# Three pairs of token tiles formed by seven block products each, with attention packed into the tiles ahead of them

## The chip, the cores and the metric

The kernel runs on one core of a Trainium2 chip. The metric is the device time of one execution in microseconds (us). Before the change the median of three runs is 853.47 us (853.21 to 854.79). About 0.2% (1.7 us) is what a measurement of this kernel can tell from no change.

## The reference

A linear attention over 8 batches, 8 heads, 576 positions and 64 features per head is followed by a two-layer network with a squared ReLU:

```python
q_s = exp(q - max(q, -1));  q_s /= sum(q_s, -1) + 1e-9      # over the 64 features
k_s = exp(k - max(k, 2));   k_s /= sum(k_s, 2) + 1e-9       # over the 576 positions
kv  = einsum('bhsd,bhse->bhde', k_s, v)
x   = einsum('bhsd,bhde->bhse', q_s, kv)   # as 4608 tokens x 512
h   = maximum(x @ w_in, 0)                 # 512 -> 2048
out = (h * h) @ w_out                      # 2048 -> 512
```

## The kernel before

Tokens are taken in nine tiles of 512. Tiles 0 to 7 hold the first 512 positions of batches 0 to 7, tile 8 gathers the last 64 positions of every batch. Every float32 operand of the network is held as a rounded high part and a rest, and each product of 128x128 by 128x512 is three matmuls (high by high, high by rest, rest by high). The weights arrive as 64-bit words and are turned into such parts during tile 0 (`scale_words`, `join_words`, `split_words`).

An ordinary tile (the loop `for t in range(WT)`, L1590, with WT = 7, so tiles 0 to 6) runs 16 columns f. `first` (L1049) forms one 128x512 piece of h from four 128-row pieces of x: 12 matmuls. ScalarE takes the ReLU (`r`), VectorE the product of h and r, ScalarE the square as the high part (`gh`), VectorE the rest (`gl`). Two columns later `second` (L1074) adds that column into four output banks: 12 matmuls. A tile is so 384 matmuls.

Tiles 7 and 8 share their work: a pair of tiles by a 2x2 split of the weights is one 2x2 block product, done with seven block products instead of eight. In the first stage (`pair_p1` to `pair_p7`, matmuls by `product`, L1264) eight pairs n of columns take 7 x 6 matmuls each; sums of weight blocks (`own_sums`, `load_weights`) and sums of x blocks (`take`, `split_x_of`) are its operands, and its results go to DRAM (`keep`). In the second stage (`product_step`, matmuls at L1780) 28 steps take 12 matmuls each; `split_step` makes the two parts of each operand from what is read back (`load_raw`), `make_t` takes differences, and `load_s` fetches sums of w_out blocks made ahead of it (`full_sums`, `add_sums`, `split_sums`, `rest_sums`, `keep_sums`). Results leave transposed by 32x32 blocks (`turned`), in 128-byte rows. A joint pair is 336 + 336 = 672 matmuls against 768 for two ordinary tiles.

Attention of batch b is made beside an earlier tile. For batches 2 to 7 it goes by head pairs p, four steps each: q in blocks (`blocks_exp`, `blocks_swap`, `blocks_norm`, `blocks_turn`), keys (`k_max`, `k_reduce` on GpSimd, `k_shift`, `k_exp`), then `kv_of` and, for two p at once, `x_two`. `ORDER` and `turns` (L1565) lay out 16 steps per tile over tiles 1 to 6, so two pairs of p per tile; `JOINED` doubles some up at the end of tile 6. `blocks_swap` exchanges the two halves of the features by four small DMAs.

Tile 0 and the start of the kernel are ordered by a planner (`Planner`, L126): it gives each instruction of attention of batches 0 and 1, of the weights and of tile 0 a start from estimated costs and due times, breaks ties by fixed seeds, and fills TensorE's waits ahead of the first tile with transposes of an identity (`fill`). From tile 1 on the order of every engine is the order of the program. All engines execute in order, and nearly all DMAs are issued by SP in that order.

Almost all instructions are recorded through the helper at L100; tile names tell them apart: `h` and `h_x` are banks of the first layer, `acc` of the second, `out` of the joint second stage, `kv` and `x` of attention.

Of the kernel before, what the change touches and what calls it, by code (L numbers as in the profile page):

```python
# [125 lines left out]
class Planner:  # L126
# [6 lines left out]
    READY, COLD, FILL, SPARE = 1.0, 0.25, 0.14, 0.2  # L133
    WAIT = 0.25

    def __init__(self):
        self.open, self.nodes, self.into, self.chain, self.boot = True, [], None, None, []
        self.marks, self.line = {}, {}
        self.due, self.dues = None, []
        self.ease = 0.0  # L140
# [19 lines left out]
    def add(self, engine, call, busy, moved, views):  # L160
# [10 lines left out]
        node.ease = self.ease  # L171
# [140 lines left out]

    def shift(self, seed):

        r = random.Random(seed)
        at, size, by = r.randrange(len(self.nodes)), r.randint(1, 40), r.gauss(0.0, 5.0)
        for n in self.nodes[at:at + size]:
            n.tail += by

    def run(self, seeds, fill):  # L320
# [4 lines left out]
        assert len(told) == len(self.nodes)  # L325
        self.open = False
        first, free = min(m.start for m in self.marks.values()), self.READY
        for n in sorted(told, key=lambda n: n.start):
            if n.engine is self.marks[0].engine and n.start <= first:
                fill(int((n.start - free - self.SPARE) / (self.FILL if free > self.READY else self.COLD)))  # L330
                free = n.end
            for call in n.calls:
                call()
# [3 lines left out]
def attention_ffn(  # L337
# [61 lines left out]
    EASE = 0.0  # L399
    EARLY = 2  # L400
# [5 lines left out]
    WT = B - 1  # L406
# [7 lines left out]
    pad2 = tiny.pool.tile([P, 68], F32, tag="pad2", name="pad2")  # L414
# [25 lines left out]
    for part in kv_parts:  # L440
# [5 lines left out]
    g_of = {  # L446
        (kind, j): dram.tile([P, 2, M], F32, tag=f"g_{kind}{j}", name=f"g_{kind}_{j}")
        for kind in KINDS for j in range(PAIRS // 2)
# [96 lines left out]
    def load_kq(b, p, which, queue=Y):  # L545
        turned = which == "k" and b == 0
        t = pair_tile(b, p, [P, C, 2, D] if turned else [P, 2, C, D], which)
# [5 lines left out]
    def load_q_blocks(b, p):  # L553

        t = att.tile([P, NG, Q], F32, tag="q", name=f"q_{b}_{p}")
# [15 lines left out]

    def load_v(b, p):
        t = pair_tile(b, p, [P, VW], "v")
# [8 lines left out]
        t = t[:, 0:C * W].rearrange("p (c w) -> p c w", c=C)  # L582
        (G if b < TB else V).memset(t[:, :, D:D + 1].only("ones"), 1.0, n=4)
        for j in range(2):
# [5 lines left out]
        made["v", b, p] = t  # L590

    def load_tail_kq(b, which, queue=Y):
# [3 lines left out]
            [P, GH, D], F32, tag=f"{which}t", name=f"{which}t_{b}", bufs=1  # L596
# [48 lines left out]
    def blocks_exp(b, p):  # L645

        t = made["q", b, p]
        st = small([P, 5, NG], "bst", f"bst_{b}_{p}", 1)
        mx = st[:, 0, :]
# [3 lines left out]
        )  # L653
        S.activation(out=t, in_=t, func=AF.Exp)
        made["bst", b, p] = st

    def blocks_swap(b, p):

        st = made["bst", b, p]
        V.tensor_reduce(out=st[:, 1, :], in_=made["q", b, p], op=ALU.add, axis=AX.X)  # L660
        for j in range(2):
            for a in range(2):
                at, of = j * D + a * Q, j * D + (1 - a) * Q
                Y.dma_start(out=st[at:at + Q, 2:4, :], in_=st[of:of + Q, 0:2, :])
        made["swap", b, p] = True

    def blocks_norm(b, p):

        t = made["q", b, p]
        st = made.pop(("bst", b, p))  # L670
        by = st[:, 4, :]
        pairs = st[:, 0:4, :].rearrange("p (k n) g -> p k n g", n=2)
        mx, sm = pairs[:, :, 0, :], pairs[:, :, 1, :]
        V.tensor_tensor(out=by, in0=st[:, 0, :], in1=st[:, 2, :], op=ALU.max)
        V.tensor_tensor(
            out=mx, in0=mx, in1=by.unsqueeze(1).broadcast_to([P, 2, NG]), op=ALU.subtract
        )
        S.activation(out=mx, in_=mx, func=AF.Exp)
        V.tensor_tensor(out=sm, in0=sm, in1=mx, op=ALU.mult)
# [5 lines left out]
        V.tensor_tensor(  # L685
            out=t, in0=t, in1=by.unsqueeze(2).broadcast_to([P, NG, Q]), op=ALU.mult
        )
# [36 lines left out]
    def k_max(b, p):  # L724
        kr = made["k", b, p]
        tl, th = tail_of(b, p)
        km = small([P, P], "km", f"km_{b}_{p}", 1)
        V.tensor_reduce(
            out=km.rearrange("p (h d) -> p h d", h=2), in_=kr.rearrange("p h c d -> p h d c"),
            op=ALU.max, axis=AX.X, n=840,  # L730
        )
# [19 lines left out]
    def k_reduce(b, p):  # L751

        km = made.pop(("km", b, p))
        kmx = small([P, P], "kmx", f"kmx_{b}_{p}")
        G.partition_all_reduce(kmx, km, channels=P, reduce_op=RED.max)
        made["kmx", b, p] = kmx
# [133 lines left out]
    def kv_product(b, p):  # L890
# [3 lines left out]
        ps = bank(f"kv_{b}_{p}", b == 0)  # L894
# [50 lines left out]
    def kv_of(b, *pairs):  # L945

        for work in (kv_product, kv_scale, kv_split):
            for p in pairs:
                work(b, p)

    def x_product(b, p, x):
# [3 lines left out]
        for i in range(2):  # L955
            cs = slice(i * SH, (i + 1) * SH)
            ps = bank(f"x_{b}_{p}_{i}", b == 0)
            with plan.together():
                for rows in heads:
# [3 lines left out]
                    )  # L963
            n = min(cs.stop, M) - cs.start
# [17 lines left out]
    def x_two(b, p, x):  # L982
# [4 lines left out]
        spare = made["spare_h"] = ps_h.tile([P, M], F32, tag="h", name=f"h_x_{b}_{p}")  # L987
# [7 lines left out]
        for n, (kv, turned) in enumerate(two):  # L995
            for at in heads:
                T.matmul(
                    out=spare[at, n * TL:(n + 1) * TL], lhsT=kv[at, at], rhs=turned[at, M:SQ],
                    start=True, stop=True,
                )  # L1000
        here = slice(p - 1, p + 1)
        one, other = (ps.rearrange("p (n c) -> p n c", n=2) for ps in both)
        S.copy(out=x[:, here, 0:HM], in_=one)
        for at, of in zip(heads, heads[::-1]):
            V.tensor_copy(out=x[at, here, HM:M], in_=other[of])
# [4 lines left out]
        if b == B - 1:  # L1010
            to = slabs[X_RAW + p // 2].bitcast(F32)[:, :, b * TL:(b + 1) * TL]
            Y.dma_start(out=to, in_=xt[:, here, :])
        elif p == NP - 1:
            Y.dma_start(out=x_tail[:, :, b * TL:(b + 1) * TL], in_=xt, kb=128)
# [17 lines left out]
    def first_part(t, f, x, p):  # L1032
        if p == 0:
# [3 lines left out]
                else made.pop("spare_h", None) or ps_h.tile([P, M], F32, tag="h", name=f"h_{t}_{f}")  # L1037
# [11 lines left out]
    def first(t, f, x):  # L1049
# [8 lines left out]
        S.activation(out=r, in_=ps, func=AF.Relu)  # L1058
        V.scalar_tensor_tensor(
# [4 lines left out]
    def split_g(t, f, ps, r):  # L1064
# [5 lines left out]
        S.activation(out=gh, in_=r, func=AF.Square)  # L1070
# [15 lines left out]
    def begin_sums(j):  # L1086

        one, two = slabs[2 * j], slabs[2 * j + 1]
        for at, slab, cols in (
            (2, one, slice(0, HM)), (6, one, slice(HM, M)), (10, two, slice(HM, M)),  # L1090
            (12, two, slice(0, HM)),
        )[:3 if j < OWN else 4]:
            Y.dma_start(out=w_sums[j][:, at:at + 2, :], in_=slab[:, :, cols].bitcast(F32))

    def full_sums(key, i):

        which, j = key
        if i == 0:
            made["full", key] = cvt.tile([P, 2, M], F32, tag="w", name=f"full_{which}{j}")
        slab = (slabs if which == "i" else slabs_o)[2 * j + i]  # L1100
        V.tensor_tensor(
            out=made["full", key][:, i, :], in0=slab[:, 0, :], in1=slab[:, 1, :], op=ALU.add
        )
# [42 lines left out]
    AT = {"b11": 4, "t1": 6, "b21": 8, "t2": 10, "t3": 12}  # L1146
# [24 lines left out]
    def load_weights(n, w, *names):  # L1171

        for name in names if w else ():
            if n >= OWN and name in SUMS:
                continue
# [3 lines left out]
    def own_sums(n, w, step):  # L1179
# [3 lines left out]
        if step == 0:  # L1183
            if n == OWN:
                a = [att.tile([P, 2, HM], F32, tag=tag, name=f"own_{tag}_{n}") for tag in "kq"]
                for i, one in enumerate(a):
                    Y.dma_start(out=one, in_=w_sums[n][:, 10 + 2 * i:12 + 2 * i, :])
            else:
                a = cvt.tile([P, 4, HM], F32, tag="w", name=f"own_a_{n}")
                Y.dma_start(out=a, in_=w_sums[n][:, 10:14, :])  # L1190
# [4 lines left out]
        a, s = made["own", n]  # L1195

        def two(name):
            return w[name][:, 0, :], w[name][:, 1, :]

        def split(name, of):  # L1200
            S.copy(out=two(name)[0], in_=of)

        def rest(name, of):
            hi, lo = two(name)
            V.tensor_tensor(out=lo, in0=of, in1=hi, op=ALU.subtract)
# [4 lines left out]
        if n == OWN:  # L1210
            a22, a11, a21, a12 = (a[i // 2][:, i % 2, :] for i in range(4))
        else:
            a22, a11, a21, a12 = (a[:, i, :] for i in range(4))
        s2, s3, s4 = (s[:, i, :] for i in range(3))
        if step == 1 and n == OWN:
            put(a22, a22, ALU.add, a11)
            put(a21, a21, ALU.add, a12)
        elif step == 1:
            put(a[:, 0:4:2, :], a[:, 0:4:2, :], ALU.add, a[:, 1:4:2, :])
        elif step == 2 and n == OWN:  # L1220
            for i, one in enumerate((a11, a12)):
                put(one, w["all"][:, 2 + 4 * i, :], ALU.add, w["all"][:, 3 + 4 * i, :])
        elif step == 2:
            put(a[:, 1:4:2, :], w["all"][:, 2:8:4, :], ALU.add, w["all"][:, 3:8:4, :])
        elif step == 3:
            put(a22, a22, ALU.add, a21)
            split("s1", a22)
            if n == OWN:
                put(s2, a22, ALU.subtract, a11)
                put(s3, a11, ALU.subtract, a21)  # L1230
            else:
                put(s[:, 0:2, :], a[:, 0:2, :], ALU.subtract, a[:, 1:3, :])
        elif step == 4:
            put(s4, a12, ALU.subtract, s2)
            rest("s1", a22)
# [8 lines left out]
    def pieces(name, t):  # L1244

        if name in AT:
# [113 lines left out]
    for work in done:  # L1360
        convert(work, 1)
    load_tail(1)
    load_kq(1, 0, "k")
    load_kq(1, 0, "q")
    load_v(1, 0)
# [3 lines left out]
    def prepare(b, p, begin=True):  # L1369

        k_max(b, p)
        if b >= TB:
            k_reduce(b, p)
            if begin:
                blocks_exp(b, p)
                if p:
                    blocks_swap(b, p)
# [633 lines left out]
```

## Time and profile before

| | |
|---|---|
| median of 3 runs | 853.47 us (853.21 to 854.79) |
| span of the profiled execution, the only time that it has | 852.0 us, 1.47 us under the median |
| TensorE matmuls busy | 841.4 us, 99% |
| VectorE busy | 603.4 us, 71% |
| ScalarE busy | 400.9 us, 47% |
| GpSimd busy | 123.6 us, 15% |
| moved by DMA | 111.79 MB, 131 GB/s |

A busy time is the union of an engine's instructions; where instructions overlap in the pipeline, the sum of their durations is larger. A matmul record lasts 0.39 us while the next begins 0.23 us after it, so the pace of TensorE is read from runs of matmuls in the chain, not from their mean durations.

### The profile page before, as it was taken

The page shows a single profiled execution, that of the slowest core. Times are in us where ns is not written, and L with a number is a line of the kernel's source. Part 1 is how long each engine was busy: PE and PEld are TensorE (multiplying, and loading weights), DVE is VectorE, ACT ScalarE, POOL GpSimd, SP SyncE. Part 2 cuts the span into 40 slices and gives each one's busy share as a digit, 9 for nine tenths or more (in the row PEclk, how much of TensorE's full clock was granted, in tenths as well). Part 3 has the DMA queues.
Part 4 walks back from the last instruction along what each step waited for, and adds up shares of the span by engine and source line. Part 5 has one row for each costly group of instructions (what it writes and reads, how often), then busy time and mean ns, then how long its engine had stood idle before and what let it go on. Part 6 is the DMA issues. An engine that isn't in the chain of part 4 may idle for free.

```text
span 852.0 us, 12804 instructions
## 1 busy us (share of the span) xinstructions
PE 841.4 (99%) x4507; PEld 682.7 (80%) x4507; DVE 603.4 (71%) x1151; ACT 400.9 (47%) x739; POOL 123.6 (15%) x143
## 2 busy tenths in 40 slices
PE   8999999999999999999999999999999999999997
PEld 7677778888888888888888888887887788888886
DVE  6889967766666667666776677676766646777985
ACT  5988844333533343424433343324433436676442
POOL 5889970000000000000000000000000000000000
PEclk9999999999999999999999999999999999999999
DMA  9993012323541444233333351133341049979465
GB/s 280 377 349 99 27 43 83 91 71 77 144 103 27 139 112 131 45 87 116 108 93 85 89 144 41 40 90 70 90 123 41 4 130 322 312 265 385 141 178 96
DMA packets 192720, 111.79 MB, mean 131 GB/s; under 512 B 130704, under 2 KB 175760, under 8 KB 192656
## 3 DMA queue, kind: packets, MB, share of 16 engines
q1 hardware_dynamic: 186736, 109.27, 43.6%
q10 hardware_dynamic: 5920, 1.71, 0.9%
q8 instruction: 35, 0.57, 0.3%
q14 instruction: 29, 0.24, 0.1%
HBM read 73.79 MB, written 36.57 MB: 130 GB/s over the span
## 4 chain that ended last, share of the span: by engine, by line
PE 88%; DMA 5%; DVE 2%; SPq 2%; ACT 1%; issue 1%; POOL 0%; DVEq 0%; ACTq 0%; POOLq 0%
PE acc L100 33%; PE h L100 30%; PE h L1268 9%; PE out L1780 6%; PE h_x L100 4%; DMA k<-in_k_dram 3%; PE kv L100 2%; PE x L100 2%; SPq L100 2%; DMA out_dram<-o 1%; DMA w<-w_sums 1%; DVE bst L100 1%; DMA bst<-bst 1%; PE qT L100 0%; DVE km L100 0%
## 5 line engine op out<-in xcount | busy, mean ns | idle before, releaser
L100 PE MATMUL acc<-w,gh 128*128 128x512 f32 x888 | 275.8, 392 | 0.0
L100 PE MATMUL h<-xh,w 128*128 128x512 f32 x800 | 264.9, 393 | 0.8 <-ACT xh L100 0.8
L100 PEld LDWEIGHTS acc<-w,gh 128*128 128x128 f32 x888 | 165.2, 188 | 36.1 <-issue 1.8
L100 PEld LDWEIGHTS h<-xh,w 128*128 128x128 f32 x800 | 150.2, 188 | 34.1 <-ACT xh L100 1.3
L100 PE MATMUL acc<-w,gl 128*128 128x512 f32 x444 | 172.9, 389 | 0.0
L100 PE MATMUL h<-xl,w 128*128 128x512 f32 x400 | 155.8, 390 | 0.0
L100 DVE TENSOR_TENSOR gl<-h,gh 128x512 fp32r<-128x512 f32 x99 | 68.1, 688 | 71.9 <-ACT gh L100 68.5
L100 ACT ACTIVATE gh<-r 128x512 fp32r<-128x512 f32 x111 | 70.0, 631 | 95.1 <-PE acc L100 93.2
L100 DVE SCALAR_TENSOR_TENSOR h<-h,r 128x512 f32<-128x512 f32 x100 | 68.9, 689 | 46.9 <-ACT r L100 45.8
L100 PEld LDWEIGHTS acc<-w,gl 128*128 128x128 f32 x444 | 83.4, 188 | 17.4
L100 ACT ACTIVATE r<-h 128x512 f32<-128x512 f32 x100 | 59.4, 594 | 68.0 <-PE h L100 67.6
L100 POOL PARTITION_ALL_REDUCE kmx<-km x24 | 16.9, 705 | 508.9 <-DVE km L100 508.9
L100 PEld LDWEIGHTS h<-xl,w 128*128 128x128 f32 x400 | 75.2, 188 | 15.2 <-DVE xl L100 0.4
L1780 PE MATMUL out<-w,w 128*128 128x512 f32 x324 | 75.7, 389 | 0.0
L1780 PEld LDWEIGHTS out<-w,w 128*128 128x128 f32 x324 | 60.8, 188 | 12.6
L100 ACT ACTIVATE q<-q 128x576 f32<-128x576 f32 (+1 forms) x32 | 21.5, 672 | 78.0 <-DVE q L100 77.0
L100 DVE TENSOR_REDUCE bst<-q 128x18 f32<-128x576 f32 x48 | 35.9, 748 | 13.9 <-ACT q L100 13.6
L100 POOL TENSOR_TENSOR w<-w,raw 128x512 int32<-128x512 int32 x32 | 41.8, 1329 | 1.7 <-DVE w L100 1.1
L100 POOL TENSOR_TENSOR w<-w,w 128x512 fp32r<-128x512 f32 x32 | 41.3, 1303 | 4.5 <-ACT w L100 3.6
L100 DVE TENSOR_TENSOR q<-q,bst 128x576 f32<-128x576 f32 x48 | 36.4, 759 | 1.7
L100 ACT ACTIVATE raw<-raw 128x1024 f32<-128x1024 f32 (+1 forms) x32 | 36.2, 1151 | 0.1
L1268 PE MATMUL h<-w,w 128*128 128x512 f32 x144 | 34.8, 389 | 0.0
(206 smaller groups left out, 1043.4 us busy)
## 6 DMA issues: line engine op xcount, KB each, us to landing
k<-in_k_dram SPq DMA_DIRECT2D x32, 256.0 KB, 2.9
raw<-in_moe_w_in_dram SPq DMA_DIRECT2D x16, 512.0 KB, 8.1
raw<-in_moe_w_out_dram SPq DMA_DIRECT2D x16, 512.0 KB, 8.6
w<-wo_sums SPq DMA_DIRECT2D x32, 256.0 KB, 3.9
w_sums<-w SPq DMA_DIRECT2D x30, 256.0 KB, 3.0
g_b<-c SPq DMA_DIRECT2D x30, 256.0 KB, 4.2
v<-in_v_dram SPq DMA_DIRECT2D x56, 128.0 KB, 3.0
out_dram<-o SPq DMA_DIRECT2D x28, 256.0 KB, 2.2
```

Source lines behind the costliest of these rows:

```text
L100: getattr(self.eng, op)(*map(real, args), **{k: real(a) for k, a in kwargs.items()})
L1268: nc.tensor.matmul(out=out.real(), lhsT=a[:, k * P:(k + 1) * P].real(), rhs=m[k].real(), start=(begin and k == 0 and i == 0), stop=(k == 1 ...
L1780: nc.tensor.matmul(out=banks[name][m].real(), lhsT=a[:, m * P:(m + 1) * P].real(), rhs=b[:, i, :].real(), start=fresh and j == i == k == 0 ...
```

## The change

`JOINT` names three pairs of tiles, (3, 4), (5, 6) and (7, 8), and WT becomes 3, so that tiles 0, 1 and 2 stay ordinary. The pair (3, 4) forms its first layer without shared products (`first_only`: 192 matmuls a tile) and only its second layer by seven block products; the pairs (5, 6) and (7, 8) do both stages so. Between pairs, `prepare_x` and `ahead_of` make the sums of the next pair's x during the last steps of a second stage, and `turned_late` puts five output transposes into the next first stage.

```diff
+    JOINT = ((B - 5, B - 4), (B - 3, B - 2), (B - 1, B))
+    WT = JOINT[0][0]
...
+            if not last:
+                if s == 4 * J + 1:
+                    prepare_x(0)
+                elif s == 4 * J + 2:
+                    prepare_x(1)
+                elif s == 5 * J:
+                    ahead_of("b11")
+                    prepare_x(2)
+                elif s == 5 * J + 1:
+                    ahead_of("b21")
...
+        prepare_x(3)
+        for j in range(J):
+            for m in range(2):
+                product_step(6 * J + j, m)
+            if j == 0:
+                w_of[0] = weights(0)
+                load_weights(0, w_of[0], "a11", "s1", "a12", "s2")
+                ahead_of("t2")
+                prepare_x(4)
+                c21 = copies(("v", "v"), out_A, "c21", att, 2)
...
+        h = ps_o.tile([P, M], F32, tag=f"o{(i * NF + s + 1) % (C - 1)}", name=f"h_{t}_{f}")
...
+    for k in range(len(JOINT)):
+        now["k"] = k
+        if k:
+            raw.clear()
+        second_products(k, first_products(k) if k else None)
```

Attention of batches 2 to 7 is laid out anew: five steps for two head pairs at once (a "pair of p"), twelve such pairs over 60 columns of tiles 1 to 4. The statistics of two p share one tile; the maximum over the four key chunks is taken by two `tensor_tensor` instead of one `tensor_reduce`; the copies of x out of its banks move from VectorE to ScalarE; from the seventh pair on the exchange of halves is four ScalarE copies (`halves_swap`) instead of four DMAs. TensorE does x of one pair and kv of the next in one burst.

```diff
+    def burst(n):
+        b, p = PAIRS_OF[n][1]
+        shared = ps_h.tile([P, M], F32, tag="h", name=f"h_kv_{b}_{p}")
...
+            x_two(*PAIRS_OF[n - 1][1], x_next if PAIRS_OF[n - 1][1][0] == TB else None, tails)
+        for i in range(2):
+            at = 2 * TL + i * W
+            kv_product(b, p - 1 + i, shared[:, at:at + W])
...
+            halves = both.rearrange("p (c h d) -> p h c d", h=2, c=2)
+            V.tensor_tensor(out=halves, in0=kr[:, :, 0:2, :], in1=kr[:, :, 2:4, :], op=ALU.max)
+            V.tensor_tensor(out=km, in0=km, in1=both[:, P:2 * P], op=ALU.max)
...
+        for at, of in zip(heads, heads[::-1]):
+            S.copy(out=x[at, here_x, HM:M], in_=other[of])
...
+    def halves_swap(row):
+        st = made["bst"]
+        for j in range(2):
+            for a in range(2):
+                at, of = j * D + a * Q, j * D + (1 - a) * Q
+                S.copy(out=st[at:at + Q, 2 + row, :, :], in_=st[of:of + Q, row, :, :])
```

In tiles 1 and 2 the product on VectorE goes: ScalarE takes ReLU, square and the rounded copy, VectorE only the rest. All ten sums of w_out and w_in blocks that stay in DRAM are made in tiles 1 and 2 (six and four); the first stage's own sums start from one load of a whole block.

```diff
+        if t:
+            S.activation(out=r, in_=r, func=AF.Square)
+            return r, None
...
+        if r is None:
+            S.copy(out=gh, in_=ps)
...
+    SUMS_AT = {
+        1: [(KEYS[i], (f, f, f + 1)) for i, f in enumerate((2, 4, 7, 9, 12, 14))],
+        2: [(KEYS[6 + i], (f, f, f + 1)) for i, f in enumerate((2, 4, 7, 9))],
     }
```

In the planner, `hold` starts DMAs whose first user is far away behind batch 1's first loads, and puts the two halves of x_product together where one TensorE instruction lies between; the number of fill transposes is worked out with other constants.

```diff
+    def hold(self, told):
+        for far in sorted({n.ahead for n in told if n.ahead}):
+            last = max(n.start for n in told if n.ahead == far)
+            held = [
+                n for n in told
+                if n.moved and not n.ahead and n.start < last
+                and min((o.start for o in n.after), default=0.0) - last > far
+            ]
...
+            if len(between) == 1 and not tags[0] & tags[1]:
+                one.start = two.start - 1e-4
```

## Rows read from the trace of the kernel before

**Rows 1.** The page: busy us, share of the span and instructions of three engines, and the clock granted to TensorE in 40 slices.

```profile
PE 841.4 (99%) x4507; PEld 682.7 (80%) x4507; DVE 603.4 (71%) x1151; ACT 400.9 (47%) x739; POOL 123.6 (15%) x143
PEclk9999999999999999999999999999999999999999
```

**Rows 2.** Busy time by stretch: the stretch and its length, then busy us and instructions of each engine, the granted clock, the share of the DMA engines and GB/s. The stretches are a piece of tile 0, tile 3 (268.81 to 361.88), the joint pair's first stage (691.30 to 768.20) and second stage (773.60 to 838.90), and two pieces in which TensorE has idle time.

```profile
645.00:660.00 15.00, 14.44 (x98) 11.78 (x97) 9.87 (x21) 4.13 (x9) 0.70 (x1) 1.00 0.24 52
...
844.30:852.00 7.70, 2.73 (x13) 1.92 (x11) 0.72 (x1) 0.00 (x0) 0.00 (x0) 0.96 0.63 103
...
40.00:110.00 70.00, 69.33 (x365) 54.52 (x364) 62.51 (x109) 57.74 (x83) 64.96 (x61) 1.00 0.51 163
268.81:361.88 93.07, 93.07 (x514) 76.11 (x513) 63.51 (x129) 35.96 (x72) 2.82 (x4) 1.00 0.35 97
691.30:768.20 76.90, 76.90 (x341) 63.67 (x340) 51.47 (x99) 48.92 (x97) 1.52 (x1) 1.00 0.84 281
773.60:838.90 65.30, 65.30 (x289) 54.07 (x289) 57.92 (x75) 32.73 (x43) 0.00 (x0) 1.00 0.64 198
```

**Rows 3.** The chain that ended last, in order of time, in tile 3: start us, length us, what, with the number of matmuls.

```profile
306.89 1.32 PE kv L100 x40
308.21 2.95 PE h L100 x12
311.16 0.68 PE acc L100 x3
311.84 1.02 PE x L100 x16
312.86 0.22 PE h_x L100 x8
313.08 7.71 PE acc L100 x33
```

**Rows 4.** The same chain in the joint pair: the long run of its first stage and of its second.

```profile
698.79 69.36 PE h L1268 x306
...
773.59 51.69 PE out L1780 x228
```

**Rows 5.** Tile 0: first the one idle time of TensorE between 42 and 131 us (the timeline of TensorE; in brackets the idle us before and its releaser), then, from the chain, x of batch 1 in two halves with other work between, and in one piece.

```profile
55.11 0.30 PE L100 MATMUL kmT<-ident,km 128*128 128x128 f32 x1 [0.67 <-DVE sm L100]
```

```profile
118.40 0.64 PE x L100 x4
119.03 0.90 PE acc L100 x3
119.93 0.64 PE x L100 x4
...
127.87 1.12 PE x L100 x8
```

**Rows 6.** VectorE in tile 3, grouped by tile and shape: count, busy us, mean ns of one, idle us before and releasers.

```profile
L100 DVE TENSOR_TENSOR gl<-h,gh 128x512 fp32r<-128x512 f32 x14 | 9.6, 688 | 11.4 <-ACT gh L100 11.1
L100 DVE SCALAR_TENSOR_TENSOR h<-h,r 128x512 f32<-128x512 f32 x14 | 9.6, 688 | 7.8 <-ACT r L100 7.6
L100 DVE TENSOR_TENSOR q<-q,bst 128x576 f32<-128x576 f32 x8 | 6.1, 758 | 0.3
L100 DVE TENSOR_REDUCE bst<-q 128x18 f32<-128x576 f32 x8 | 6.0, 748 | 2.3 <-ACT q L100 2.3
L100 DVE TENSOR_REDUCE km<-k 128x128 f32<-128x512 f32 x4 | 4.2, 1060 | 0.0
L100 DVE STREAM_TRANSPOSE qT<-q 128x576 f32<-128x576 f32 x4 | 3.1, 778 | 0.1
...
L100 DVE COPY x<-x 64x512 f32<-64x512 f32 x4 | 2.8, 688 | 0.9 <-PE x L100 0.9
...
L100 DVE TENSOR_TENSOR sums_o<-full_o 128x256 f32<-128x256 f32 x4 | 1.7, 418 | 0.0
L100 DVE TENSOR_TENSOR bst<-bst 128x36 f32<-128x36 f32 x8 | 1.6, 196 | 1.3 <-ACT bst L100 1.2
```

**Rows 7.** ScalarE in tile 3, grouped in the same way.

```profile
L100 ACT ACTIVATE gh<-r 128x512 fp32r<-128x512 f32 x17 | 10.7, 632 | 16.9 <-PE acc L100 16.6
L100 ACT ACTIVATE r<-h 128x512 f32<-128x512 f32 x14 | 8.3, 594 | 11.7 <-PE h L100 11.7
```

**Rows 8.** The timeline of VectorE in the joint second stage: a difference in two halves, and the rest of a whole operand.

```profile
779.78 1.29 DVE L100 TENSOR_TENSOR raw_b<-raw_b,raw_b 128x512 f32<-128x512 f32 x2
780.99 1.22 DVE L100 TENSOR_TENSOR w<-w,w 128x1024 fp32r<-128x1024 f32 x1
```

**Rows 9.** The chain that ended last beside tile 6, where attention of one p and the next follow each other: start us, length us, what.

```profile
633.10 0.77 DVE bst L100
...
643.84 0.50 SPq L100
...
659.04 0.80 PE kv L100 x20
```

**Rows 10.** The DMA view of the last 27 us: packets and bytes, and the shares of the 16 engines that the packets of two queues took.

```profile
DMA packets 17862, 2.79 MB, mean 103 GB/s; under 512 B 17202, under 2 KB 17860, under 8 KB 17860
...
q1 hardware_dynamic: 13572, 2.25, 43.2%
q10 hardware_dynamic: 4288, 0.53, 12.2%
```

More of the change, by code (lines that the diff above doesn't have):

```diff
@@ L994, in x_two @@
                     )
[L995 to L1000, printed above, removed]
[L1001 removed]
+        here = slice(p - 1, p + 1)
+        if x is None:
+            closed = PAIRS_OF.index(((b, p - 1), (b, p))) >= CLOSE - 1
+            x = closing[1] if closed else att.tile([P, 2, M], F32, tag="qn", name=f"x_{b}_{p}", bufs=1)
+            here_x = slice(0, 2)
+        else:
+            here_x = here
         one, other = (ps.rearrange("p (n c) -> p n c", n=2) for ps in both)
[L1003 to L1005 removed]
         if p == 1:
@@ L1194, in own_sums @@
             made["own", n] += [cvt.tile([P, 4, HM], F32, tag="w", name=f"own_s_{n}")]
-        a, s = made["own", n]
-        def two(name):
-            return w[name][:, 0, :], w[name][:, 1, :]
+        (row, other), s = made["own", n]
+        a11, a12, a21, a22 = row[:, 0, :], row[:, 1, :], other[:, 0, :], other[:, 1, :]
+        s1, s2, s3, s4 = (s[:, i, :] for i in range(4))
+        two = w["all"][:, 2:8:4, :], w["all"][:, 3:8:4, :]
         def split(name, of):
-            S.copy(out=two(name)[0], in_=of)
+            S.copy(out=w[name][:, 0, :], in_=of)
@@ L1214, in own_sums @@
[L1214 to L1222, printed above, removed]
+        if step == 1:
+            put(s1, a21, ALU.add, a22)
@@ L1223, in own_sums @@
         elif step == 2:
-            put(a[:, 1:4:2, :], w["all"][:, 2:8:4, :], ALU.add, w["all"][:, 3:8:4, :])
+            put(s2, s1, ALU.subtract, a11)
+            put(s3, a11, ALU.subtract, a21)
+            put(s4, a12, ALU.subtract, s2)
         elif step == 3:
[L1226 to L1232, printed above, removed]
+            S.copy(out=two[0], in_=row)
@@ L1746, in attention_ffn, with place, set_of @@
     banks = {}
+    def place(name, i=0):
+        return slabs[PLACES[now["k"]][name] + i]
+    def set_of(s):
+        if s < len(steps) - 1:
+            return ((slabs[0], slabs[1]), (slabs[14], slabs[15]), (place("t1"), place("t1", 1)))[s % 3]
+        if now["k"] < len(JOINT) - 1:
+            return [cvt.tile([P, 2, M], F32R, tag="w", name=f"last_{i}") for i in range(2)]
+        return place("b21"), place("b21", 1)
     def weight(name, n):
@@ L1759, in split_step @@
         name, j = steps[s]
[L1760 removed]
+        hi, lo = set_of(s)
         src = raw[name, j]
```

1050 lines of the change are left out of this document (683 added, 367 removed), and 3 rows, old and new, of the table PLACES.

## The prediction

> **What bounds the kernel now.** I read the page first: TensorE is busy 99% of the span, and its clock is granted in full throughout [rows 1]. Busy matmuls prove little when their records overlap, so the second view is busy time by stretch: tile 3, both joint stages and a piece of tile 0 show TensorE full or nearly so while VectorE stands at 68% (63.51 of 93.07), 67%, 89% and 89% [rows 2]. The third is the chain that ended last: through tile 3 it is one matmul after the other [rows 3], and in the joint stages 306 matmuls take 69.36 us and 228 take 51.69 us [rows 4]. Both are 0.2267 us each: the pace of a 128x512 matmul with nothing waited for. So a matmul that disappears is worth 0.2267 us, provided VectorE and ScalarE still deliver. The idle time that is left lies in the start, 0.67 us in tile 0 [rows 5], 0.56 us where attention is late beside tile 6, and some 5 us at the very end (7.70 less 2.73) [rows 2].
>
> **Term 1, the matmuls.** Before: 7 x 384 + 672 = 3360. After: tiles 0 to 2 give 3 x 384 = 1152, the plain first layers of tiles 3 and 4 2 x 192 = 384, their joint second stage 336, two full joint pairs 2 x 672 = 1344, in all 3216. The 144 that go are worth 144 x 0.2267 = 32.6 us [rows 4]. The count follows from the loops, so this term has no range of its own.
>
> [...] The measured pace is used.
>
> **Term 2, bursts.** Attention's small matmuls cost more than their own time: the 12 matmuls behind kv take 2.95 us and not 2.72, the 33 behind x 7.71 and not 7.48 [rows 3], so each return to full-size matmuls costs 0.23 us. Before there are two returns for each pair of p, 24 in all; after, x of one pair and kv of the next stand together, and with the last x 13 are left. 11 x 0.23 = 2.5 us less. What kv and x themselves take (1.32 + 1.02 + 0.22 us) stays. If a burst must wait for a bank the gain is gone; I take the whole, since what it waits for is due four steps ahead (term 5).
>
> **Term 3, tile 0.** The loads of batch 1 that now pass far weights bring the key maximum earlier, whose lateness left the 0.67 us. The halves of x that are put together save 0.64 + 0.90 + 0.64 - 1.12 - 3 x 0.2267 = 0.38 us [rows 5], in one place. Together 1.0 us. The weights that are held back are covered by GpSimd, which is what paces their conversion (64.96 of 70 us busy [rows 2]). Should the order come out badly, another wait of the size of the old one is the cost: the term lies between -1.0 and +0.7.
>
> **Term 4, the late stretch.** Beside tile 6 attention's steps were doubled up and TensorE idled 0.56 us [rows 2]. That layout is gone: -0.6.
>
> **Term 5, the other engines (taken at nothing).** I sum VectorE by rows. An ordinary tile from 1 on keeps `gl` only: 16 x 0.688 = 11.0 us, and some 3.4 for splits and stores; the product of 0.688 a column goes [rows 6]. The price is on ScalarE: ReLU, square and copy, 16 x (0.594 + 0.632 + 0.62) = 29.5 us [rows 7], far under a tile. A sum of weights takes two additions, four of 0.418 and two rests, 4.4 us [rows 6]; tile 1 has six and one whole block, 27.8 us. A pair of p took 16.7 us on VectorE in tile 3 (all of its groups there added up); off go the copies of x (1.4), half of the small statistics (1.2) and the difference between a 1.06 us reduction and an estimated 0.7 us for two maxima (0.7): 13.4 us [rows 6]. Tile 1 has 3.2 pairs: 42.9. Sum 85 us, in a tile of 16 x 5.44 + 3.2 x 2.8 = 96 us: 89%. Tiles 3 and 4 last 192 x 0.2267 + 3.2 x 2.8 = 52.5 us each, with 46 us and less of VectorE: 87%. In a second stage that another pair follows: 26 splits of 1.25, 16 differences of 1.26 [rows 8], five pairs of sums and transposes (6.2), and the next pair's eight differences and ten rests of 0.69 (12.4): 71 us of 28 x 2.72 = 76.2, 93%. A following first stage has 51.5 + 8 squares + 5 transposes + 2 = 62 us of 76 [rows 2, 6].
>
> So VectorE stands at 87 to 93% where it stood at 67 to 89%. TensorE was full beside VectorE at 89% over 65 and 70 us [rows 2]. The sums of durations overstate the union by 5% (67 against 63.5 in tile 3), except in the second stage, whose pace is from a timeline. Then the waits: in order, tiles 3 and 4 give a pair of p five columns, 5 x 2.72 + 2.8 = 16.4 us. Following one pair through (shift, exponential, sum, exchange on ScalarE, weights, norm, transpose, then kv and x), ScalarE holds a ReLU back by at most some 1.5 us, where three rotating banks allow 5.4, and k, q and kv are ready 5 us ahead of their burst. SP issues some 22 DMAs in that time at 0.50 us each [rows 9]; a column's store is issued a step late, so that nothing waits behind it. At steps 20 to 22 of a second stage the next pair's sums are queued ahead of split 24 and later; I get a backlog of 4.4 us, against three steps (8 us) of lead. So I cost this at nothing, with the rival below for the other end.
>
> **Term 6, the seams.** Three are new: tile 4 to its second stage, and two from a second to a first stage. The trace has a seam into a first stage and one into a second, both without idle time [rows 2]; the other end is the drain at the end, 5 us each. I take 1 us each, 3.0 in all, near the first rows since operands are made 3 to 7 steps ahead, but not zero because VectorE has no slack there. Bounds 0 and 15.
>
> **Sum.** 852.0 - 32.6 - 2.5 - 1.0 - 0.6 + 3.0 = 818.3 us of span, and 1.5 us as in the run before between span and median: 819.8 us.
>
> **Rivals.**
> *VectorE sets the pace in the dense stages.* If it can't hold more than the 89% that the trace shows over a long stretch [rows 2], each second stage that another pair follows takes 71 / 0.89 = 80 us, 3.6 more; at 85%, 83.5 (+7.3 each), and tile 1 (85 / 0.85 = 100) 4 and tiles 3 and 4 1.6 each. That is 827 to 842; 830 is its middle. Against: at 89% TensorE doesn't wait for it at all, so the 89% is demand and not a limit.
> *Output packets fill the DMA engines.* 24 of the transposed outputs leave in 128-byte rows where 8 did. In the last 27 us 17862 packets took 55.4% of the engines' time, so 2048 packets take 1.7 us [rows 10]. A first stage was at 84%, 64.6 us [rows 2]; five outputs add 8.6, and the weights that own sums no longer fetch (18 x 256 KB at the stage's 335 GB/s) take off 14. Were the loads not saved in time, both first stages would slip by 8.6 us: 837.
> [...]
> *Attention stays a serial chain, and the kernel is slower.* Beside tile 6 one p and the next took from 633.10 to 659.04, 26 us, through DMA exchange and key load [rows 9]. A pair that took so long in tiles 3 and 4 would hold TensorE 9.5 us beyond its 16.4, for 5.8 pairs: 55 us, 875. It decides for slower from 22 us a pair. Against: keys are fetched a pair ahead, and the exchange there is no DMA.
>
> **Chances.** Forecast (815 to 825) 0.70; VectorE's pace 0.20; packets 0.05; serial chain 0.03; something between that eats the gain 0.02. Range: low 814.5 (no seam and a little more in tile 0), high 833 (forecast, most of VectorE's case, part of packets): 8 in 10 and some. About 0.2%, 1.7 us, is what a measurement can tell from no change. Faster 0.95, same 0.01, slower 0.04.
>
> **What would show it.** Right: the chain in tiles 3 and 4 and all joint stages at 0.2267 us a matmul, 13 returns of 0.23 us, TensorE's busy time near 806 us. Term 5 falls if TensorE idles on `xl`, `w` or `kv` from VectorE at steps 20 to 27 or behind bursts, term 6 if idle time of over 1 us stands at a seam, the packets if DMA share is at 1 where a matmul waits for a ring or raw load. Wrong altogether if tiles 3 and 4 last over 60 us each.

## The result and the profile after

The changed kernel takes 820.41 us (median of five runs, 819.46 to 822.12) against 854.79 us of the kernel before beside it (853.21 to 855.45): a ratio of 0.9603, 95% interval 0.9583 to 0.9622. A second set gave 820.93 us (four runs) and 0.9592, 0.9566 to 0.9619. The forecast was 819.8 us. The profiled execution spans 818.6 us where that of before spans 852.0: 33.4 us less.

First the page of the kernel after: busy us, share of the span and instructions of each engine, and the granted clock in 40 slices. These answer to [rows 1].

```profile
PE 805.5 (98%) x4362; PEld 653.2 (80%) x4362; DVE 650.9 (80%) x1202; ACT 502.7 (61%) x932; POOL 126.6 (15%) x143
PEclk9999999999999999999999999999999999999999
```

TensorE has 35.9 us less to do; VectorE went from 71% to 80%, ScalarE from 47% to 61%. TensorE still bounds, with its clock granted at 1.00 in every stretch below.

Busy time by stretch of the kernel after, in the columns of [rows 2]: tile 1, tile 3 with the first 1.2 us of tile 4, two pieces near the end of tile 4, then from the joint stages a second, a first, a second and the last second, and the end.

```profile
132.46:227.60 95.14, 94.75 (x554) 77.06 (x553) 78.63 (x172) 56.92 (x111) 6.68 (x7) 1.00 0.60 166
323.08:376.00 52.92, 52.92 (x391) 42.79 (x390) 36.69 (x86) 37.49 (x90) 5.06 (x7) 1.00 0.82 224
410.00:418.00 8.00, 8.00 (x46) 6.41 (x48) 6.71 (x15) 6.72 (x15) 0.00 (x0) 1.00 1.03 303
418.00:426.00 8.00, 8.00 (x84) 6.48 (x77) 2.60 (x5) 4.51 (x13) 0.00 (x0) 1.00 1.03 309
440.70:508.90 68.20, 68.20 (x301) 56.42 (x302) 59.80 (x77) 38.16 (x55) 0.00 (x0) 1.00 0.70 217
508.92:585.10 76.18, 76.18 (x338) 63.08 (x337) 58.38 (x114) 45.15 (x95) 1.30 (x1) 1.00 0.74 233
585.08:661.47 76.39, 76.39 (x338) 62.97 (x337) 67.11 (x90) 39.25 (x54) 0.00 (x0) 1.00 0.69 229
737.76:803.00 65.24, 65.24 (x290) 54.01 (x289) 55.62 (x71) 31.90 (x41) 0.00 (x0) 1.00 0.64 216
810.80:818.60 7.80, 3.12 (x14) 2.25 (x12) 0.72 (x1) 0.00 (x0) 0.00 (x0) 1.00 0.61 100
```

The joint stages are filled to the last tenth with VectorE at 77% to 88% (58.38 of 76.18, 67.11 of 76.39). The two 8 us pieces near the end of tile 4 are the odd ones: the DMA engines are full (1.03), and in the second of them VectorE is busy for only 2.60 of 8 us.

The chain that ended last, of the kernel after, in order of time, with the columns of [rows 3, 4]: a burst in tile 3 with the piece behind it, and three joint stages.

```profile
334.34 0.87 PE x L100 x14
335.21 1.32 PE h_kv L100 x40
336.52 13.85 PE h L100 x60
...
508.92 73.44 PE h L1414 x324
582.36 2.72 PE out L2006 x12
585.08 2.72 PE h L1414 x12
587.80 73.67 PE out L2006 x324
661.47 73.57 PE h L1414 x324
```

73.44 / 324 is 0.2267 us, the pace of before. x and kv stand together, and behind them is one return: 13.85 - 60 x 0.2267 = 0.25 us. At the seam of 582 us the stages interleave without a gap.

The timeline of TensorE in the kernel after shows the idle time that is new (in brackets: idle us before, and its releaser).

```profile
394.68 0.50 PE L100 MATMUL h<-xh,w 128*128 128x512 f32 x1 [0.53 <-ACT c L100]
...
398.25 0.50 PE L100 MATMUL h<-xh,w 128*128 128x512 f32 x1 [0.55 <-ACT c L100]
...
430.20 0.50 PE L2006 MATMUL out<-w,w 128*128 128x512 f32 x1 [1.56 <-ACT c L100]
```

All three wait for a ReLU of ScalarE, two in the middle of tile 4 and one where its second stage begins. Besides, there is one of 0.39 us at 222.97, near the end of tile 1, for a high part `gh` of ScalarE.

**Where 33.4 us came from.** By the same stage limits in both traces: matmuls -32.6; bursts -2.3; tile 1 starts at 132.46 instead of 134.65, -2.2; new stalls +5.0; the last drain 0.3 shorter (4.68 against 4.97 us of idle time). The 1.0 us that is left of the gain holds the 0.56 us of idle time beside tile 6, and about 0.4 us that I don't assign. The +5.0 are 1.0 in tiles 1 and 2 (190.62 - 768 x 0.2267 - 15.56 of bursts), 1.6 in the middle of tile 4 and 2.4 at its seam, each wait with the restart behind it.

### The profile page after: what moved, and what is told of

Its sections match the earlier page's. It is cut to its first block, busy times and chain, and to the rows that moved or that the text cites. A ratio compares the mean times of both kernels' runs of the same rounds, so it can differ in the third digit from the quotient of the medians.

```text
span 818.6 us, 13021 instructions
## 1 busy us (share of the span) xinstructions
PE 805.5 (98%) x4362; PEld 653.2 (80%) x4362; DVE 650.9 (80%) x1202; ACT 502.7 (61%) x932; POOL 126.6 (15%) x143
## 4 chain that ended last, share of the span: by engine, by line
PE 88%; DMA 3%; ACT 3%; DVE 2%; issue 1%; SPq 1%; POOL 0%; ACTq 0%; DVEq 0%; POOLq 0%
PE out L2006 26%; PE h L100 22%; PE h L1414 19%; PE acc L100 15%; PE h_kv L100 2%; PE x L100 2%; DMA q<-in_q_dram 1%; SPq L100 1%; DMA g_b<-c 1%; PE kv L100 1%; DVE w L100 0%; DMA out_dram<-o 0%; ACT closing L100 0%; DMA v<-in_v_dram 0%; PE qT L100 0%
## 5 line engine op out<-in xcount | busy, mean ns | idle before, releaser
L2006 PE MATMUL out<-w,w 128*128 128x512 f32 x942 | 222.0, 390 | 1.8 <-ACT c L100 1.6
L100 PE MATMUL h<-xh,w 128*128 128x512 f32 x640 | 209.0, 394 | 1.9 <-ACT c L100 1.1
L2006 PEld LDWEIGHTS out<-w,w 128*128 128x128 f32 x942 | 176.4, 188 | 40.3 <-ACT c L100 2.0
L100 PE MATMUL acc<-w,gh 128*128 128x512 f32 x376 | 117.4, 393 | 0.4 <-ACT gh L100 0.4
L100 PEld LDWEIGHTS acc<-w,gh 128*128 128x128 f32 x376 | 69.5, 188 | 16.0 <-issue 0.9
L100 PE MATMUL acc<-w,gl 128*128 128x512 f32 x188 | 73.4, 390 | 0.0
L1414 PEld LDWEIGHTS h<-w,w 128*128 128x128 f32 x288 | 54.1, 188 | 11.2
L100 ACT CAST w<-w 128x1024 fp32r<-128x1024 f32 (+1 forms) x49 | 48.5, 998 | 23.4 <-PE out L2006 12.0
L100 DVE TENSOR_TENSOR w<-w,w 128x1024 fp32r<-128x1024 f32 (+1 forms) x33 | 36.7, 1122 | 20.0 <-ACT w L100 20.0
L1414 PE MATMUL h<-w,ring 128*128 128x512 f32 x192 | 46.2, 390 | 0.0
```

Source lines behind the costliest of these rows:

```text
L100: getattr(self.eng, op)(*map(real, args), **{k: real(a) for k, a in kwargs.items()})
L1414: nc.tensor.matmul(out=out.real(), lhsT=a[:, k * P:(k + 1) * P].real(), rhs=m[k].real(), start=(begin and k == 0 and i == 0), stop=(k == 1 ...
L2006: nc.tensor.matmul(out=banks[name][m].real(), lhsT=a[:, m * P:(m + 1) * P].real(), rhs=b[:, i, :].real(), start=fresh and j == i == k == 0 ...
```

## Experiments

The sum was met, but three terms were not: the start gave twice what it should, tile 4 has waits in a place costed at nothing, and its seam costs 2.4 us where the two later ones cost nothing. Theories: (a) the start's gain is the held loads, or else the other count of fill transposes; (b) tile 4's waits come from VectorE, crowded at the boundary of tiles 3 and 4, or else from ScalarE's own load of ReLU, square and copies; (c) the seam's wait comes from a late load, or else from the same lag of ScalarE. Beside these, bursts and the slack of VectorE were measured by themselves. Where one time stands for a kernel, the stage lengths in its trace are what is compared.

**The old count of fills.** The planner's constants for the fills go back, so that 24 and not 17 stand ahead of `ek`.

```diff
-    READY, COLD, FILL, SPARE = 1.0, 0.2, 0.14, 0.2
+    READY, COLD, FILL, SPARE = 1.0, 0.25, 0.14, 0.2
```

> The changed kernel with the planner's old constants for the fill transposes. Theory: of the 2.2 us by which tile 1 starts earlier than before, 1.0 us comes from shorter fills: 24 of them stood ahead of the first transposes of ek before (9.38 to 13.12), 17 after. Then ek starts at about 13.1 us, not 12.0, tile 1 about 1.0 us later than 132.46. Rival (the loads of batch 1 and their order gave all of it): ek and tile 1 stay where they are within 0.2 us.

Measured: 822.66 us, span 820.2. Timeline of TensorE in this kernel:

```profile
9.36 3.33 PE L1699 MATMUL idle<-ident 128*128 128x128 f32 x24
12.53 0.60 PE L100 MATMUL ek<-ident,k 128*128 128x128 f32 x4
```

`ek` stands right behind the fills, and tile 1 starts at 132.81. Kernels with the new fills and held loads start it between 132.17 and 133.13, so the 0.35 us between this kernel and the kernel after are within the spread of the start: a miss for the theory that the fills made the gain.

**No held loads.**

```diff
-    AHEAD = 24.5, 30.0
+    AHEAD = 0.0, 0.0
```

> The changed kernel without the passing of far weights by batch 1's first loads; the fills and the joined halves of x stay. Theory: the 0.67 us of idle time ahead of kmT near 54 us come back, nothing else moves; tile 1 starts at about 133.1 us instead of 132.46. Rival (the early loads take DMA time from weights and are worth nothing): no idle time there and tile 1 within 0.2 us.

Measured: 822.94 us, span 820.3, tile 1 at 133.06, 0.6 us later than after but still inside that spread. The wait for the key maximum is back (timeline of TensorE, this kernel; its first line is TensorE's last wait ahead of it), where the kernel after has `kmT` at 53.29 us without a wait:

```profile
35.27 0.50 PE L100 MATMUL h<-xh,w 128*128 128x512 f32 x1 [0.82 <-ACT xh L100]
...
53.86 0.30 PE L100 MATMUL kmT<-ident,km 128*128 128x128 f32 x1 [0.68 <-DVE sm L100]
```

So the held loads do what they should. Their worth shows once the spread is taken off: from the matmul of that first line to tile 1 it takes 97.79 us here, and 96.85 to 96.91 in all eleven profiles with held loads (96.88 after, from 35.58 to 132.46). That is 0.9 us, the wait and the restart behind it. But `kmT` is 1.2 us earlier here than in [rows 5] with the same wait, which the next run takes up.

**The kernel before, profiled again.**

> The kernel before, profiled once more, for the start. In the first profile of it the 24 fill transposes ahead of ek took 3.90 us and ek began at 13.12 us; with the same count in the changed kernel they took 3.33 and ek began at 12.53. Theory fills (they stand ahead of a ready ek whatever the run): ek again at 12.5 us or later, right behind the fills, without idle time, and tile 1 at 134.0 to 134.7 us. Rival (the 1.0 us was the spread of one start): ek before 12.3 us and tile 1 at 133.7 us or earlier.

Measured: 854.05 us, span 852.3. Timeline of TensorE:

```profile
12.03 0.66 PE L100 MATMUL ek<-ident,k 128*128 128x128 f32 x4 [0.42 <-ACT k L100]
...
55.07 0.30 PE L100 MATMUL kmT<-ident,km 128*128 128x128 f32 x1 [1.58 <-DVE sm L100]
```

This execution began as early as the kernel after does (that wait for `xh` ends at 35.62, where the first profile has 36.56), and 0.9 us more of waiting at `kmT` took all of it back: tile 1 starts at 134.60, as in the first profile. The key load of batch 1, not the start, sets `kmT` at 55.1. So the fills can't be the cause; what frees `kmT` is also what lets an earlier start count. The kernel without held loads issues that key load at 42.28 us, and the two profiles of before at 43.52 and 43.25, though SP's order up to there is the same; why SP stands a us earlier was not settled.

**x and kv apart in tiles 1 and 2.**

```diff
+                    if c == 1 and todo and todo[1] == 3:
+                        burst_x(todo[0])
                     if c == 2 and todo and todo[1] == 3:
-                        burst(todo[0])
+                        burst_kv(todo[0])
```

> The changed kernel with x and kv apart again in tiles 1 and 2: x behind the second output bank, kv behind the third. Five bursts fall apart, so if each return to full-size matmuls costs 0.23 us, tiles 1 and 2 (190.62 us from 132.46 to 323.08) take 1.1 to 1.2 us more. Rival (the cost goes with the small matmuls and not with the return): no more than 0.3 us.

Measured: 822.71 us, span 820.9; tiles 1 and 2 last 191.63 us (132.81 to 324.44) against 190.62 (190.61 to 190.66 in the nine other profiles with held loads). That is 1.0 us for five more returns, 0.2 each: the price of term 2, seen by itself.

**Tile 4's squares left out.**

```diff
-            if i or f % 2:
+            if f % 2:
                 S.activation
```

> The changed kernel with the eight squares of even columns of tile 4 left out, so that part of the output is that of other numbers. Theory ScalarE: in tile 4 ScalarE's order (ReLU, square, attention) is what holds banks back, and 8 x 0.63 us less of it remove the two waits of 0.5 us near 394 and 398 us and shorten the wait at the seam to the second stage (1.8 us idle near 429); tiles 3 and 4 take 107.88 us now and would take 104 to 105.5. Theory VectorE or DMA (what ScalarE waits for is late itself): 107.5 or more, the waits stay.

Measured: 819.82 us, span 816.9. The two waits in the middle become one of 1.14 us at 398.52, so their sum stays; the wait at the seam is gone. That hints at ScalarE's load at the seam, and speaks against it in the middle. From the start of tile 3 to steady `out` matmuls it takes 105.71 us, between the bounds of both theories. But the seam also changes by itself: that length is 107.88 us in after, 107.06 in its second profile and 106.42 in the kernel without held loads, which has the same code there. So the length of a seam alone decides little; it has to be read together with its releaser.

**The raw loads of `b12` later in tile 4**, at columns 11 and 12 and not 5 and 6.

```diff
-        if f == 5:
+        if f == 11:
             raw_x = att.tile([P, 4, M], F32, tag="x_next", name="raw_b12_0")
...
-        elif f == 6:
+        elif f == 12:
             load_raw("b12", 2, temp
```

> The changed kernel with the three loads of b12 parts (1.5 MB) in tile 4 six columns later, behind the last q loads in SP's order. The last part of tile 4 (from the burst near 401 us) shows DMA engines full, stores that land after 6 us, and a q load that comes 2.8 us late for VectorE. Theory DMA: with the loads out of the way the q load comes in time, ScalarE's order catches up and the idle time at the seam to the second stage (1.3 to 1.8 us in three of four profiles so far, 0.3 in one) is under 0.3 us; tiles 3 and 4 take 106.4 us or less, not 107.9. Theory ScalarE (its own work is too much there): the seam stays at 1 us or more.

Measured: 818.53 us, span 816.7. The first `out` matmul comes at 428.18 without idle time ahead of it; tiles 3 and 4 take 105.39 us to there, against 107.12 in after. The two waits in the middle stay (0.53, 0.54 us). What changed is seen ahead of the seam. In the kernel after, the timelines of SP, VectorE and ScalarE:

```profile
412.01 3.59 SPq L100 DMA_DIRECT2D g_b<-c  x1
415.69 2.08 SPq L100 DMA_DIRECT2D closing<-in_q_dram  x4
```

```profile
420.49 0.76 DVE L100 TENSOR_REDUCE bst<-closing 128x18 f32<-128x576 f32 x1 [2.80 <-DMA closing<-in_q_dram]
```

```profile
422.07 0.69 ACT L100 ACTIVATE closing<-closing 128x576 f32<-128x576 f32 x1 [1.93 <-DVE closing L100]
...
424.43 0.58 ACT L100 ACTIVATE c<-h 128x512 f32<-128x512 f32 x1
```

And the timeline of SP with the loads later:

```profile
412.87 1.96 SPq L100 DMA_DIRECT2D closing<-in_q_dram  x4
```

A store takes 3.59 us of SP while the DMA engines are full (1.03 from 410 to 418 us, where the kernel with the loads later has 0.68), the q load behind it goes out at 415.69 and not at 412.87, VectorE waits 2.80 us for it, ScalarE's exponential 1.93 us for VectorE, and the ReLU that is queued behind that comes some 7 us after its matmuls. Only the DMA engines are full in this chain; the rest is three queues in order, each held by the one ahead.

The sizes fit as well. In the eight profiles of kernels that have tile 4 as the kernel after has it, the wait of VectorE for this load and the idle time that the seam's first `out` matmul has ahead of it are 2.80 and 1.56, 2.44 and 1.19, 2.31 and 1.11, 2.29 and 1.03, 1.97 and 0.74, 1.78 and 0.52, 1.60 and 0.48, 1.29 and none: beyond some 1.2 us of slack, the load's lateness comes out at the seam one for one. So in this kernel the late load sets the seam's wait, and not the waits in the middle; and the slack depends on what ScalarE has behind it, for without tile 4's squares a wait of 1.49 us costs nothing. Moving the loads has a small price of its own: in the two kernels that do it, and in no other, TensorE waits near 447 us, in the second stage, for a `w` of VectorE (0.31 us here).

**Tile 4 takes x parts 1 to 3 from tile 3.**

```diff
-                split_next(later_x, t + 1, 1, 2, 3)
+                later_x.extend(x[1:])
```

> The changed kernel in which tile 4 takes three of its four x parts from tile 3 (part of the output is that of other numbers), so that the three splits at the boundary (three copies on ScalarE, three rests on VectorE) are left out. The waits of 0.53 and 0.55 us near 394 and 398 us stand in every profile so far. Theory boundary: the three splits and two attention steps fall into one column there, and the lag that they make is still there 10 us later; without them both waits vanish and tiles 3 and 4 get 1.4 to 1.7 us shorter. Rival (the attention chain of tile 4 has that period anyway): the waits stay at 0.8 us or more in sum.

Measured: 815.92 us, span 814.1. From the start of tile 3 to steady `out` matmuls it takes 103.88 us, against 107.88 in after: 4.0 us, more than twice what was expected, since the seam's wait went too. Of the three copies that are left out, two are ScalarE's and one is VectorE's, not all three ScalarE's as expected. The chain of this kernel through tile 4:

```profile
385.57 13.85 PE h L100 x60
...
401.98 13.85 PE h L100 x60
...
418.38 8.41 PE h L100 x36
426.79 8.34 PE out L2006 x36
```

No gap is left: 32 x 2.72 + 6 x 2.8 = 103.84 us is what tiles 3 and 4 take with nothing waited for. Where the lag starts is on VectorE, at the boundary (its timeline in the kernel after):

```profile
373.70 0.43 DVE L100 CAST xh<-x 128x512 fp32r<-128x512 f32 x1 [1.92 <-PE h L100]
374.16 0.69 DVE L100 TENSOR_TENSOR xl<-x,xh 128x512 fp32r<-128x512 f32 x1
375.04 1.37 DVE L100 TENSOR_TENSOR xl<-x,xh 128x512 fp32r<-128x512 f32 x2 [0.18 <-ACT xh L100]
376.32 0.15 DVE L100 TENSOR_SCALAR ks<-h_kv 128x1 f32<-128x1 f32 x1
```

The split waits 1.92 us for tile 3's last column to be done with the buffers of x, then takes 2.6 us in all, and two steps of attention are queued behind it: `ks` comes at 376.32 us, and at 371.70 without the splits. 18 us later that is still a ReLU at 394.03 where the other kernel has it at 389.99. The run took away the wait and the splits together; which of the two halves weighs more was not tried apart. At the seam the load is late in this kernel too (timeline of VectorE):

```profile
416.14 0.75 DVE L100 TENSOR_REDUCE bst<-closing 128x18 f32<-128x576 f32 x1 [2.48 <-DMA closing<-in_q_dram]
```

Without the lag of the boundary, 2.48 us of lateness cost nothing. So the seam's wait takes both, the late load and the lag, and either cure removes it.

**Squares of tile 3 put off.** ScalarE's squares of columns 13 and 15 of tile 3 move into the second stage.

```diff
-            if i or f % 2:
+            if i or f % 2 and f < NF - 4:
                 S.activation
...
+                if k == 0 and differences[s] == (2, 3):
+                    square_raw("b22", 3)
```

> The changed kernel with the squares of columns 13 and 15 of tile 3 (b22, two of 0.63 us on ScalarE, at the boundary to tile 4) moved into the second stage, ahead of the difference that uses them. Theory boundary with ScalarE as the one that lags: the two waits in tile 4 (1.08 us in sum) fall to 0.5 us or less. Rival (VectorE is the one that lags at the boundary, with three rests of 0.68 us and the attention steps): the waits stay at 0.9 us or more.

Measured: 820.65 us, span 818.9. Timeline of TensorE:

```profile
394.44 0.50 PE L100 MATMUL h<-xh,w 128*128 128x512 f32 x1 [0.54 <-ACT c L100]
...
398.01 0.50 PE L100 MATMUL h<-xh,w 128*128 128x512 f32 x1 [0.55 <-ACT c L100]
```

Both waits stay as they were, so these 1.3 us of ScalarE's load at the boundary aren't what makes them, though every one of them names ScalarE.

**Additions to VectorE in the second stages**, one 128x512 addition at every fourth step, and at every step, from the fourth on:

```diff
+            if s >= 3 and s % 4 == 3:      # second kernel: if s >= 3
+                V.tensor_tensor(out=dosed, in0=wide_ones, in1=wide_ones, op=ALU.add)
```

> The changed kernel with an addition of 128x512 that nothing uses (about 0.69 us) on VectorE behind every fourth step of the three second stages, five or six in each. Theory of the prediction (VectorE has slack in a second stage: 67.1 us of 76.4 busy in the middle one): nothing is longer by more than 0.3 us a stage. Rival (VectorE already sets the pace there): each stage takes 3 us more.

> The same addition behind every step from the fourth on, 21 in each second stage, 14.5 us of VectorE. If VectorE becomes the bound only when its own work fills the stage, the middle stage takes 67.1 + 14.5 = 81.6 us instead of 76.4, and the three together some 12 to 18 us more. If it is the bound already: 14.5 us each, 43 in all. If other slack hides it (the order lets VectorE lag by three steps): under 6 us in all.

Measured: 822.98 us (span 821.2) with some 4 us added to each stage, 844.40 us (span 842.5) with some 14. The first adds 1.1 us to the first second stage, 1.8 to the middle one and 0.1 to the last; the second 8.0, 9.4 and 7.0. Timeline of TensorE in the middle stage with the smaller addition:

```profile
602.79 3.04 PE L2006 MATMUL out<-w,w 128*128 128x512 f32 x12 [0.34 <-DVE w L100]
...
652.16 6.01 PE L2006 MATMUL out<-w,w 128*128 128x512 f32 x25 [0.32 <-issue]
658.58 2.80 PE L2006 MATMUL out<-w,w 128*128 128x512 f32 x11 [0.40 <-DVE w L100]
```

And busy time by stretch with the larger one, in that stage:

```profile
595.30:678.40 83.10, 77.59 (x326) 61.10 (x325) 77.04 (x109) 37.11 (x52) 0.00 (x0) 0.98 0.63 201
```

VectorE was not the bound: the 24 us in all are little over half of the 43 us added, though more than the 12 to 18 expected. It had some slack, less than I thought: 4 us fit into the last stage and not into the middle one. That one loses 1.8 us, with one wait in its first quarter and two at its end, where VectorE has the next pair's sums queued ahead of the stage's own operands. With the larger addition, where it did bound, it ran at 93% (77.04 of 83.10).

**The kernel after, a second time, and both cures.** The last kernel holds the later loads of `b12` and the put-off squares together.

> The changed kernel once more, as the measure for the next two: 819.5 to 822.1 us; the waits of 0.53 and 0.55 us in tile 4 stand, the idle time at the seam is between 0.3 and 1.8 us.

> Both moves that cost no work: b12's loads six columns later and the two squares in the second stage. The seam's idle time goes (1 to 1.8 us and 0.8 us of refill), and by the first theory half of the waits in tile 4: 1.5 to 3 us under the changed kernel's own time in the same call. By the rival only the seam: 1 to 2 us.

Measured: 820.93 us (820.11 to 821.51, four runs each) and 819.34 (818.50 to 821.41), ratios to before of 0.9592 (0.9566 to 0.9619) and 0.9580 (0.9546 to 0.9615). In the kernel with both moves the seam's idle time is gone, with the first `out` matmul at 428.67 us; the two waits in the middle stay at 0.53 and 0.51, as the rival has it. The 1.6 us are of the seam's size, but the two ranges overlap, and the one run with the later loads alone (818.53) lies inside the range of both moves: what the moves gain is hardly separated by these runs.

The second profile of the kernel after also has a wait that the first has not, at the seam from the first second stage to the next first stage (timeline of TensorE):

```profile
510.21 5.73 PE L1414 MATMUL h<-w,w 128*128 128x512 f32 x24 [0.57 <-DMA w<-w_sums]
```

The kernel with the squares put off has two there, 0.76 and 0.31 us. The sums of weights that they wait for are issued by SP behind twelve output stores, from 503.65 and 505.05 us on. That seam has no slack to speak of, then; what holds the stores back was not tried.

## Why the prediction was right

It was right in its main term and its mechanism, and close to 0.6 us because smaller errors cancelled.

**Term 1 held**: 32.6 us predicted, and the long runs of the joint stages took 0.2267 to 0.2275 us a matmul (324 in 73.44 to 73.67 us, 300 in 68.25). TensorE's busy time is 805.5 us (near 806 was said).

**Term 2 held**: 2.3 us of 2.5, and 0.2 us a return when they were put back.

**Term 3 failed in size**: 2.2 us, outside its bounds of -1.0 and +0.7. I priced the wait at `kmT` by its 0.67 us in one profile. That figure is only what was left between an early or late start and a fixed key load; in the second profile of before it is 1.58. What the step should have asked is when the key load lets `kmT` go (55.1 in both profiles of before; after, nothing is waited for and it comes at 53.3). From the last wait ahead of `kmT`, at 35 to 37 us, to tile 1 it takes 98.09 and 98.98 us in the two profiles of before, 97.79 without held loads and 96.88 after. So the held loads are worth 0.9 us against the first profile and some 0.9 more against the second, and 0.3 are left for the joined halves of x (0.4 by their rows). In the first pair of profiles the other 1.0 us of the 2.2 is the earlier start itself, 35.58 against 36.56. Kernels with the same code there spread over 35.26 to 36.26, so that part is luck of the pair; but before, an early start was lost again at `kmT`, and after it isn't.

**Term 4** can't be separated from the end: at most 1.0 us with what isn't assigned, 0.6 predicted.

**Term 5 failed in tile 4**: 1.6 us of waits costed at nothing, and some 1.0 in tiles 1 and 2. Its sums were on the safe side (tile 1: 85 predicted, 78.63 measured; the middle second stage 71 and 67.11), and the share of VectorE was never the matter. My walk followed one pair of p through a steady tile. It had no tile boundary in it, and so not the split that waits for the matmuls of the tile before and holds two steps of attention. It let ScalarE hold a ReLU back by 1.5 us at most; near the seam one came some 7 us after its matmuls. Its backlog at steps 20 to 27 of a second stage was nearer to the edge than the 4.4 of 8 us said: 4 us more, spread out, cost 1.8 us.

**Term 6 failed in shape**: 3 x 1.0 predicted, 2.4 and twice 0 measured in the first profile, and in the second 1.6, some 0.8 and 0 (waits with the restarts behind them). That the sum of 3.0 came near 2.4 is luck. I looked for the price in VectorE, and at the first seam it lay in a load that was late, on top of the lag from the boundary: SP was costed at 0.50 us an issue, with stores behind which nothing waits, and one store held it for 3.59 us with a load behind it.

**The rivals.** VectorE as the pace falls: TensorE was full beside 88% over 76 us, and the overloaded stage shows VectorE at 93%, above the 85 to 89% that the rival took for a limit. (The middle of its 827 to 842 is 834.5, not 830.) Packets as a bound of the joint stages fall, with the DMA engines' share at 0.64 to 0.74 over each of them; nor did the rival's own sum reach that far, for 64.6 + 8.6 = 73.2 us still fit into a stage of 76. But in tile 4, at 1.03, full DMA engines did delay a load, for 1.7 us by the run with later loads, in a place that I had not looked at. No output store is issued there, so it isn't the rival's mechanism; whether small packets or plain bytes filled the engines there was not tried, and moving loads was enough to be rid of the delay. The serial chain falls: tiles 3 and 4 last 107 us together, and not over 120.

## What to carry to other kernels

Where TensorE is full, price a removed matmul by the pace of long runs in the chain, and then spend the care on boundaries: walk the queues over each change of tile, for here a VectorE split that waited 1.92 us for buffers held what was queued behind it, and a wait of 0.53 us showed 18 us later under ScalarE's name. A stage's busy shares say little about such a place; the small test is to take away one load or one step and see if the wait goes. An idle time of one profile isn't the worth of its cause: ask what time the late operand itself allows.

## What the runs showed of the hardware

`PARTITION_ALL_REDUCE` on GpSimd takes 843 ns in the mean after and 705 before (24 of each). VectorE's share isn't the difference: 19 of the 24 after take 0.70 to 0.81 us like all of those before, and the other five, 1.12 or 1.60 us, are those that begin during VectorE's additions for the sums of weights (`full_o` at 157.67, 184.97, 215.43 and 251.95 us, `full_i` at 281.50). No wait of TensorE in the kernel after names it (the one on GpSimd, 1.6 us, is for `ident`), and the cause was not tried.

Four 128x128 transposes took 0.66 us in some executions and 1.12 in others at the same place, 8.3 to 8.5 us into the span, and 24 fill transposes 2.78 to 3.90 us, with the granted clock at 1.00 in all of these stretches. The row of the granted clock doesn't show what made them differ, and no run here settled it.

A return from attention's small matmuls to full-size ones cost 0.2 us with each of the bursts measured: 0.23 behind kv and behind x in [rows 3], 0.25 behind both after, 0.2 in the run that put five of them back.
